# A gated mix of linear attention and a GEGLU feed-forward: order, halves and queues of the first loads, and q beside k

## The chip, the core and the metric

The kernel runs on one core of a Trainium2 chip. The core has TensorE (PE in the profile, with its weight loads as PEld), VectorE (DVE), ScalarE (ACT), GpSimd (POOL) and SyncE (SP), which run side by side and wait for each other by semaphores. SP and ACT issue the DMAs here. The metric is the device time of one launch in microseconds (us), the median over several launches.

## The reference

```python
def _A_ref(x, wqkv, wo):
    qkv = (x @ wqkv).reshape(B, S, 3, H, Dh).transpose(2, 0, 3, 1, 4)
    q, k, v = qkv[0], qkv[1], qkv[2]
    phi = lambda t: jnp.where(t > 0, t + 1, jnp.exp(t)) + 1e-6
    pq, pk = phi(q), phi(k)
    kv = jnp.einsum("bhsd,bhse->bhde", pk, v)
    z = jnp.einsum("bhsd->bhd", pk)
    num = jnp.einsum("bhqd,bhde->bhqe", pq, kv)
    den = jnp.einsum("bhqd,bhd->bhq", pq, z)[..., None] + 1e-6
    return (num / den).transpose(0, 2, 1, 3).reshape(B, S, D) @ wo

def _B_ref(x, w_gate, w_up, w_down):
    return (_gelu(x @ w_gate) * (x @ w_up)) @ w_down

x = A_x                      # S = 2048 rows, D = 640, H = 32 heads of 20, F = 1728
g = _sigmoid((x * gate_w).sum(-1, keepdims=True))
return g * _A_ref(x, A_wqkv, A_wo) + (1 - g) * _B_ref(x, B_w_gate, B_w_up, B_w_down)
```

All inputs and the output are bf16.

## The kernel before

The 2048 rows of x are 16 tiles of 128 rows; the 640 columns are 5 chunks of 128 (index k). Every matmul with x needs x transposed, with its columns on the partitions: this is xT. There are two ways into it. For the first NXN = 3 tiles, x is loaded as it is (L337) and T(i) (L396) transposes it with five TensorE transposes into a PSUM bank, from where a DVE copy (L406) takes it into xT. The other 13 tiles come by a transposing DMA each, issued by SP (load_xT, L340).

The work then goes in stages: phi(k) and phi(q) (L391 to L490); the products of phi(k) with x, from which kv and z are derived (MM and ME, from L495); the feed-forward's gate and up matmuls (G, L595), with the rest of the attention woven in (KV, W2, N); the output (FA, FB_half and FB). Only the first stage and its loads are touched by the change.

In the first stage, KM(i, ks) (L411) does, for tile i and each chunk k in ks, a pair of matmuls with the same weights, of 512 and 128 columns of wk; five pairs make a tile of k. QM(i) (L424) does the same with wq, whose chunk has one more column: the gate weights, put there by a small transpose and a DVE copy (L464 to L468). Each tile's result lies in a pair of PSUM banks (slot, L393): four pairs of banks in turn, though the first three tiles use the first three pairs and tile 3 the last. phi1(n) (L437) is ScalarE's Exp of it, with a Tanh of the gate column for a q tile; phi2(n) (L447) is two DVE instructions that make phi and store it, which frees the banks.

Everything is written down by hand in program order. P.op puts an instruction into its engine's list with the buffers it reads and writes; the planner works out the waits from these. Every engine runs its list in order, so an instruction that waits holds up all that is behind it on its engine. Waits are by whole buffers as named: the five chunks of wk are five names, wq is one, each tile of xT is one.

The order at the start: ACT issues the gate column, then the five chunks of wk (L334 to L336). SP issues x tiles 0 to 2 (L337, L338), then the 13 transposing DMAs (L345), then the rest of x in two pieces (L347 to L350), wg, wu, wv, wo. These later loads have no waits but SP's own order. On TensorE, warm (L382) first does a few matmuls with constants, whose results nobody reads, and then (L457 to L474):

```python
warm(6, 512); T(0); warm(2, 128); T(1); warm(2, 128)
KM(0, [0]); T(2)        # then the gate column's transpose
KM(1, [0])
for k in range(1, KC):
    KM(0, [k]); KM(1, [k]); KM(2, [k - 1])
KM(2, [KC - 1])
```

After that come k of tiles 3 to 15 and q of tiles 0 to 15, each with all five chunks (L475 to L481). wq is loaded as one transfer from ACT's queue, issued behind phi of tile 3 (L483). late_constants (L366), put down after tile 6, is work for POOL that waits for nothing but POOL.

Of the kernel before, what the change touches and what calls it, by code (L numbers as in the profile page):

```python
# [14 lines left out]
NT = S // 128  # L15
KC = D // 128
# [3 lines left out]
EPS = 1e-6  # L20
XW = 656

NXN = 3

class _Res:
    __slots__ = ("name", "writer", "readers", "excl", "lo", "hi", "idx", "fresh")
# [133 lines left out]
def bass_gated_mix__linear_attn_block__geglu_ffn__prompt_kernel(  # L160
# [24 lines left out]
    R_XT = take(KC * S)  # L185
# [36 lines left out]
    with (  # L222
# [8 lines left out]
        with contextlib.ExitStack() as stack:  # L231
# [65 lines left out]
            r_xone = P.sb("xone", R_XN, R_XN + NT * XW)  # L297
            r_pk = [P.sb("pk%d" % i, R_PK + i * 640, R_PK + (i + 1) * 640) for i in range(NT)]
            r_xT = [P.sb("xT%d" % i, R_XT, R_XT + KC * S) for i in range(NT)]
            r_wk = [P.sb("wk%d" % k, R_WK + k * 640, R_WK + (k + 1) * 640) for k in range(KC)]  # L300
            r_wq = P.sb("wq", R_WQ, R_WQ + KC * XW)
            r_gcol = P.sb("gcol", R_WQ, R_WQ + KC * XW)
            r_wv = P.sb("wv", R_WV, R_WV + KC * 640)
            r_wg = P.sb("wg", R_WG, R_WG + KC * 1664)
# [24 lines left out]
            def dma_in(dst, src, writes, reads=(), eng="sp"):  # L329
                P.op(eng, lambda e, dst=dst, src=src: e.dma_start(dst, src),  # L330
                     reads=reads, writes=writes, dma=new_dma_key())


            dma_in(gw_sb[0:5, :], gate_w.rearrange("(k p) -> k p", p=128), [r_gw], eng="act")  # L334
            for k in range(KC):
                dma_in(wk[:, k, :], A_wqkv[k * 128:(k + 1) * 128, 640:1280], [r_wk[k]], eng="act")  # L336
            for i in range(NXN):  # L337
                dma_in(x_aug[:, i, 0:640], A_x[0, i * 128:(i + 1) * 128, :], [r_xn[i]])  # L338

            def load_xT(i, after=()):  # L340
                P.op("sp", lambda e: e.dma_start_transpose(xT[:, :, i * 128:(i + 1) * 128],
                                                           A_x[0, i * 128:(i + 1) * 128, :]),
                     reads=list(after), writes=[r_xT[i]], dma=new_dma_key())

            for i in range(NXN, NT):  # L345
                load_xT(i)
# [44 lines left out]
            SLOTS = [(0, 1), (2, 3), (4, 5), (6, 7)]  # L391

            def slot(n):  # L393
                return SLOTS[n] if n < 3 else SLOTS[n % 4]

            def T(i):  # L396
                tb = 6 + i % 2

                def fn(e):
                    last = None  # L400
                    for k in range(KC):
                        last = e.transpose(psb[:, tb, k * 128:(k + 1) * 128],
                                           x_aug[:, i, k * 128:(k + 1) * 128], ident)
                    return last
                P.op("pe", fn, reads=[r_xn[i], r_ident], writes=[bank[tb]])
                P.op("dve", lambda e: e.tensor_copy(  # L406
                    xT[:, :, i * 128:(i + 1) * 128],
                    psb[:, tb, 0:640].rearrange("p (k s) -> p k s", k=KC)),
                    reads=[bank[tb]], writes=[r_xT[i]])

            def KM(i, ks):  # L411
                b0, b1 = slot(i)

                def fn(e):
                    last = None
                    for k in ks:
                        lhs = xT[:, k, i * 128:(i + 1) * 128]
                        e.matmul(ps[:, b0, :], lhs, wk[:, k, 0:512], start=(k == 0), stop=(k == KC - 1))  # L418
                        last = e.matmul(ps[:, b1, 0:128], lhs, wk[:, k, 512:640],  # L419
                                        start=(k == 0), stop=(k == KC - 1))  # L420
                    return last
                P.op("pe", fn, reads=[r_xT[i]] + [r_wk[k] for k in ks], writes=[bank[b0], bank[b1]])

            def QM(i):  # L424
                b0, b1 = slot(NT + i)

                def fn(e):
                    last = None
                    for k in range(KC):
                        lhs = xT[:, k, i * 128:(i + 1) * 128]  # L430
                        e.matmul(ps[:, b0, :], lhs, wq[:, k, 0:512], start=(k == 0), stop=(k == KC - 1))  # L431
                        last = e.matmul(ps[:, b1, 0:129], lhs, wq[:, k, 512:641],  # L432
                                        start=(k == 0), stop=(k == KC - 1))
                    return last
                P.op("pe", fn, reads=[r_xT[i], r_wq, r_gcol], writes=[bank[b0], bank[b1]])

            def phi1(n):  # L437
                b0, b1 = slot(n)
                m = n % 4
                P.op("act", lambda e: e.activation(e_buf[m], ps_flat[:, b0 * 512:b0 * 512 + 640], ACT.Exp),  # L440
                     reads=[bank[b0], bank[b1]], writes=[r_e[m]])
                if n >= NT:
                    i = n - NT
                    P.op("act", lambda e: e.activation(eg[:, i:i + 1], ps[:, b1, 128:129], ACT.Tanh, scale=0.5),
                         reads=[bank[b1]], writes=[r_eg[i]])

            def phi2(n):  # L447
                b0, b1 = slot(n)
                m = n % 4
                P.op("dve", lambda e: e.tensor_scalar(e_buf[m], e_buf[m], 1.0, EPS, ALU.min, ALU.add),  # L450
                     reads=[r_e[m]], writes=[r_e[m]])
                dst, r_dst = (pk[n], r_pk[n]) if n < NT else (pq[n - NT], r_pq[n - NT])
                P.op("dve", lambda e: e.scalar_tensor_tensor(  # L453
                    dst, ps_flat[:, b0 * 512:b0 * 512 + 640], 1.0 + EPS, e_buf[m], ALU.add, ALU.max),
                    reads=[bank[b0], bank[b1], r_e[m]], writes=[r_dst])

            warm(6, 512)  # L457
            T(0)
            warm(2, 128)
            T(1)  # L460
            warm(2, 128)
            KM(0, [0])
            T(2)
            P.op("pe", lambda e: e.transpose(psb[:, 7, 0:5], gw_sb[0:5, :], ident[0:5, 0:5]),  # L464
                 reads=[r_gw, r_ident], writes=[bank[7]])
            P.op("dve", lambda e: e.tensor_copy(wq[:, :, 640:641],
                                                psb[:, 7, 0:5].rearrange("p (k o) -> p k o", o=1)),
                 reads=[bank[7]], writes=[r_gcol])  # L468
            KM(1, [0])
            for k in range(1, KC):  # L470
                KM(0, [k])
                KM(1, [k])
                KM(2, [k - 1])
            KM(2, [KC - 1])  # L474
            for n in range(2 * NT):  # L475
                if n >= NT:
                    QM(n - NT)
                elif n >= 3:
                    KM(n, list(range(KC)))
                phi1(n)  # L480
                phi2(n)  # L481
                if n == 3:
                    dma_in(wq[:, :, 0:640], A_wqkv[:, 0:640].rearrange("(k p) w -> p k w", p=128), [r_wq],  # L483
                           eng="act")
                if n == 6:
                    late_constants()
            P.op("dve", lambda e: e.tensor_scalar(gg, eg, 0.5, 0.5, ALU.mult, ALU.add),
                 reads=r_eg, writes=[r_g])
# [316 lines left out]
```

## Time and profile before

| | us |
|---|---|
| median of 14 runs (276.66 to 278.55) | 277.27 |
| the profiled execution | 277.81 |
| span of the profiled execution | 276.5 |
| q and k tiles on TensorE, to the start of L502 | 51.37 |
| ACT issues of wk, five, first at | 1.40 |
| SP issues of the 13 transposing DMAs, first at 2.19, together | 21.09 |
| Exp of a tile (L440), mean of 32 | 0.703 |
| the two DVE instructions of a tile (L450, L453), means | 0.324 and 0.825 |
| DVE copy of a transposed tile (L406) | 0.49 |

The span is the time from the first to the last instruction that the profiler saw; what the launch adds lies around it. Times in the timeline are counted from the start of the span. A time in brackets behind an instruction is how long its engine was idle before it, with what released it. A DMA's time to landing counts from its issue until its semaphore says that all has arrived.

### The profile page before, as it was taken

The numbers are of one execution on the slowest core, as the hardware profiler recorded it, in microseconds if no ns is written. First come the engines' busy times: TensorE is split into PE (matmuls) and PEld (weight loads), VectorE is DVE, ScalarE is ACT, GpSimd is POOL, SyncE is SP. The second block draws the span as 40 slices with busy tenths as digits, with TensorE's granted clock in tenths as the row PEclk, the third lists the DMA queues.
The fourth block names the chain that finished last, engine by engine and source line by source line (L and its number), as shares of the span: only waits on it lengthen the run. The fifth ranks groups of instructions, "written<-read, shape, count | busy, mean of one in ns | idle before, by whom it ended". The sixth has DMA issues, their size and how long they took to land.

```text
span 276.5 us, 4070 instructions
## 1 busy us (share of the span) xinstructions
PE 271.9 (98%) x1696; PEld 140.2 (51%) x1696; DVE 138.5 (50%) x233; ACT 78.2 (28%) x132; POOL 26.1 (9%) x28
## 2 busy tenths in 40 slices
PE   7999999999999999999999999999999999999997
PEld 3455555555545444444444444444555555555553
DVE  1398888610243324999999999625100122212223
ACT  1354555310332354222232222323555100000000
POOL 5000000000000400332423322000000000000000
DMA  7998998002030212121221212390000011111111
GB/s 170 165 185 217 396 401 287 14 0 50 1 71 2 47 50 71 24 47 30 43 48 24 47 34 40 55 314 14 0 0 2 3 47 47 47 50 47 50 39 56
DMA packets 36401, 22.38 MB, mean 81 GB/s; under 512 B 25760, under 2 KB 34976, under 8 KB 36384
## 3 DMA queue, kind: packets, MB, share of 16 engines
q1 hardware_dynamic: 34997, 20.49, 27.9%
q10 hardware_dynamic: 1386, 1.64, 2.5%
q8 instruction: 13, 0.21, 0.4%
q14 instruction: 5, 0.03, 0.0%
HBM read 13.11 MB, written 2.62 MB: 57 GB/s over the span
## 4 chain that ended last, share of the span: by engine, by line
PE 95%; DMA 3%; ACTq 1%; DVE 0%; issue 0%
PE ps L595 41%; PE ps L738 20%; PE ps L701 6%; PE ps L431 6%; PE ps L502 6%; PE ps L418 6%; DMA pool<-in_A_wqkv_dram 3%; PE ps L504 2%; PE ps L432 2%; PE ps L702 2%; PE ps L570 2%; PE ps L419 1%; PE ps L722 1%; ACTq L330 1%; PE ps L616 1%; PE ps L632 1%
## 5 line engine op out<-in xcount | busy, mean ns | idle before, releaser
L595 PE MATMUL ps<-pool 128*128 128x512 bf16 x520 | 113.7, 379 | 0.0
L595 PEld LDWEIGHTS ps<-pool 128*128 128x128 bf16 x520 | 50.4, 98 | 60.0 <-issue 0.3
L738 PE MATMUL ps<-pool 128*128 128x512 bf16 (+1 forms) x416 | 57.2, 299 | 0.0
L603 DVE TENSOR_TENSOR pool<-ps,pool 128x512 bf16<-128x512 f32 x52 | 35.7, 687 | 33.6 <-PE ps L595 30.4
L601 ACT ACTIVATE pool<-ps 128x512 f32<-128x512 f32 x52 | 31.0, 597 | 72.5 <-PE ps L595 72.5
L749 DVE SCALAR_TENSOR_TENSOR pool<-ps,pool 128x512 bf16<-128x512 f32 (+1 forms) x32 | 16.2, 547 | 63.8 <-PE ps L738 63.8
L738 PEld LDWEIGHTS ps<-pool 128*128 128x128 bf16 x416 | 31.9, 98 | 25.2 <-issue 1.1
L647 POOL TENSOR_TENSOR pool<-pool 128x640 f32<-128x640 bf16 x16 | 22.5, 1408 | 141.0 <-DMA pool<-z_row 87.8
L440 ACT ACTIVATE pool<-ps 128x640 bf16<-128x640 f32 x32 | 22.3, 703 | 24.0 <-PE ps L419 14.4
L453 DVE SCALAR_TENSOR_TENSOR pool<-ps,pool 128x640 bf16<-128x640 f32 x32 | 26.4, 825 | 2.2
L655 DVE TENSOR_TENSOR pool<-pool 128x640 bf16<-128x640 bf16 x16 | 23.1, 1442 | 0.6
L418 PE MATMUL ps<-pool 128*128 128x512 bf16 x80 | 22.5, 383 | 0.6 <-DMA pool<-in_A_wqkv_dram 0.5
L431 PE MATMUL ps<-pool 128*128 128x512 bf16 x80 | 21.9, 379 | 0.0
L502 PE MATMUL ps<-pool 128*128 128x512 bf16 x80 | 21.9, 379 | 0.0
L701 PE MATMUL ps<-pool 128*128 128x512 bf16 x80 | 21.8, 379 | 0.0
L419 PE MATMUL ps<-pool 128*128 128x128 bf16 x80 | 17.6, 220 | 0.0
L432 PE MATMUL ps<-pool 128*128 128x129 bf16 x80 | 17.6, 220 | 0.0
L504 PE MATMUL ps<-pool 128*128 128x129 bf16 x80 | 17.6, 220 | 0.0
L702 PE MATMUL ps<-pool 128*128 128x128 bf16 x80 | 17.5, 219 | 0.0
L706 ACT ACTIVATE pool<-ps,pool 128x640 f32<-128x640 f32 x16 | 12.7, 793 | 9.2 <-PE ps L702 9.2
L450 DVE TENSOR_SCALAR pool<-pool 128x640 bf16<-128x640 bf16 x32 | 10.4, 324 | 7.4 <-ACT pool L440 5.7
L418 PEld LDWEIGHTS ps<-pool 128*128 128x128 bf16 x80 | 7.9, 98 | 10.3 <-DMA pool<-in_A_wqkv_dram 0.8
(51 smaller groups left out, 130.2 us busy)
## 6 DMA issues: line engine op xcount, KB each, us to landing
out_dram<-pool SPq DMA_DIRECT2D x15, 160.0 KB, 1.8
pool<-in_B_w_gate_dram SPq DMA_DIRECT2D x1, 2080.0 KB, 13.7
pool<-in_B_w_up_dram SPq DMA_DIRECT2D x1, 2080.0 KB, 18.4
pool<-in_A_x_dram SPq DMA_DIRECT2D x1, 1280.0 KB, 8.4
pool<-in_B_w_down_dram SPq DMA_DIRECT2D x1, 1120.0 KB, 5.7
pool<-in_A_wo_dram SPq DMA_DIRECT2D x6, 160.0 KB, 8.8
pool<-in_B_w_down_dram SPq DMA_DIRECT2D x1, 960.0 KB, 8.1
pool<-in_A_wqkv_dram ACTq DMA_DIRECT2D x5, 160.0 KB, 5.0
```

The costliest lines, as they stand in the source:

```text
L418: e.matmul(ps[:, b0, :], lhs, wk[:, k, 0:512], start=(k == 0), stop=(k == KC - 1))
L431: e.matmul(ps[:, b0, :], lhs, wq[:, k, 0:512], start=(k == 0), stop=(k == KC - 1))
L432: last = e.matmul(ps[:, b1, 0:129], lhs, wq[:, k, 512:641], start=(k == 0), stop=(k == KC - 1))
L453: P.op("dve", lambda e: e.scalar_tensor_tensor(dst, ps_flat[:, b0 * 512:b0 * 512 + 640], 1.0 + EPS, e_buf[m], ALU.add, ALU.max), reads=[ba ...
L502: e.matmul(ps[:, bs[n], :], lhs, x_aug[:, i, 0:512], start=(i == 0), stop=(i == NT - 1))
L504: last = e.matmul(ps[:, bt, n * 129:(n + 1) * 129], lhs, x_aug[:, i, 512:641], start=(i == 0 and n == 0), stop=(i == NT - 1), skip_group_c ...
L595: last = e.matmul(ps[:, b, :], w[:, k, fc * 128:(fc + 1) * 128], xT[:, k, j * 512:(j + 1) * 512], start=(k == 0), stop=(k == KC - 1))
L601: P.op("act", lambda e: e.activation(ge[n], ps[:, gb, :], ACT.Gelu_apprx_tanh), reads=[bank[gb]], writes=[r_ge[n]])
L603: P.op("dve", lambda e: e.tensor_tensor(hT[fc][:, j * 512:(j + 1) * 512], ps[:, ub, :], ge[n], ALU.mult), reads=[bank[ub], r_ge[n]], write ...
L655: P.op("dve", lambda e: e.tensor_tensor(pq[i].rearrange("p (h d) -> p h d", h=32), pq[i].rearrange("p (h d) -> p h d", h=32), den[n].unsqu ...
L701: e.matmul(ps[:, b0, :], lhs, w2[:, m, 0:512], start=(m == 0), stop=(m == KC - 1))
L738: last = e.matmul(dst, lhs, wd[:, fc, c0:c0 + cn], start=False, stop=(fc == NFC - 2), skip_group_check=True)
```

## The change

NXN becomes 2, so tile 2 comes by a transposing DMA and there are 14 of these. The early loads (x tiles 0 and 1, the chunks of wk, and wq in two pieces of two and three chunks) are each split into partitions 0 to 63, issued by SP, and 64 to 127, issued by ACT (halves). Their order on both queues is x0, wk0, x1, wk1 to wk4, on ACT the gate column, then wq. wq is thus issued ahead of the transposing DMAs, no longer behind phi of tile 3. Each half has a name of its own to wait for, and wq has one for each chunk.

T takes a list of chunks and a bank: tile 0 is transposed in two pieces, the first chunk alone. A list, seq, gives the order of tiles: k0, k1, q0, q1, and from tile 2 on k and q of a tile in turn; slot goes by the position in it. The order of the first pairs is written anew, the gate column's transpose (gate_col) moves behind the fourth chunk of k1, and QM takes a list of chunks. There are five heating matmuls instead of six and one group of two small ones instead of two.

```diff
--- before.py
+++ after.py
@@ -20,7 +20,8 @@
 EPS = 1e-6
 XW = 656
 
-NXN = 3
+NXN = 2
@@ -297,8 +298,12 @@
             r_xone = P.sb("xone", R_XN, R_XN + NT * XW)
             r_pk = [P.sb("pk%d" % i, R_PK + i * 640, R_PK + (i + 1) * 640) for i in range(NT)]
             r_xT = [P.sb("xT%d" % i, R_XT, R_XT + KC * S) for i in range(NT)]
+            r_xn_hi = [P.res("xnh%d" % i) for i in range(NXN)]
+            r_wk_hi = [P.res("wkh%d" % k) for k in range(KC)]
+            r_wq_hi = [P.res("wqh%d" % k) for k in range(KC)]
+            r_x0a = P.sb("x0a", R_XT, R_XT + 128)
             r_wk = [P.sb("wk%d" % k, R_WK + k * 640, R_WK + (k + 1) * 640) for k in range(KC)]
-            r_wq = P.sb("wq", R_WQ, R_WQ + KC * XW)
+            r_wq = [P.sb("wq%d" % k, R_WQ + k * XW, R_WQ + k * XW + 640) for k in range(KC)]
             r_gcol = P.sb("gcol", R_WQ, R_WQ + KC * XW)
...
@@ -331,16 +336,42 @@
                      reads=reads, writes=writes, dma=new_dma_key())
 
 
+
+            def load_x(i, eng):
+                dma_in(x_aug[:, i, 0:640], A_x[0, i * 128:(i + 1) * 128, :], [r_xn[i]], eng=eng)
+
+            def load_wk(k, eng):
+                dma_in(wk[:, k, :], A_wqkv[k * 128:(k + 1) * 128, 640:1280], [r_wk[k]], eng=eng)
+            def halves(dst, src, r_lo, r_hi):
+                dma_in(dst[0:64], src[0:64], r_lo)
+                dma_in(dst[64:128], src[64:128], r_hi, eng="act")
+
+            def load_x(i):
+                halves(x_aug[:, i, 0:640], A_x[0, i * 128:(i + 1) * 128, :], [r_xn[i]], [r_xn_hi[i]])
+
+            def load_wk(k):
+                halves(wk[:, k, :], A_wqkv[k * 128:(k + 1) * 128, 640:1280], [r_wk[k]], [r_wk_hi[k]])
+
+            def load_wq(k0, k1):
+                halves(wq[:, k0:k1, 0:640],
+                       A_wqkv[k0 * 128:k1 * 128, 0:640].rearrange("(k p) w -> p k w", p=128),
+                       r_wq[k0:k1], r_wq_hi[k0:k1])
+
+            load_x(0)
+            load_wk(0)
+            load_x(1)
+            for k in range(1, KC):
+                load_wk(k)
             dma_in(gw_sb[0:5, :], gate_w.rearrange("(k p) -> k p", p=128), [r_gw], eng="act")
-            for k in range(KC):
-                dma_in(wk[:, k, :], A_wqkv[k * 128:(k + 1) * 128, 640:1280], [r_wk[k]], eng="act")
-            for i in range(NXN):
-                dma_in(x_aug[:, i, 0:640], A_x[0, i * 128:(i + 1) * 128, :], [r_xn[i]])
-
-            def load_xT(i, after=()):
+            load_wq(0, 2)
+            load_wq(2, KC)
+
+            def load_xT(i):
                 P.op("sp", lambda e: e.dma_start_transpose(xT[:, :, i * 128:(i + 1) * 128],
                                                            A_x[0, i * 128:(i + 1) * 128, :]),
-                     reads=list(after), writes=[r_xT[i]], dma=new_dma_key())
+                     writes=[r_xT[i]], dma=new_dma_key())
 
             for i in range(NXN, NT):
                 load_xT(i)
@@ -391,25 +422,29 @@
             SLOTS = [(0, 1), (2, 3), (4, 5), (6, 7)]
 
             def slot(n):
-                return SLOTS[n] if n < 3 else SLOTS[n % 4]
-
-            def T(i):
-                tb = 6 + i % 2
-
+                return SLOTS[n % 4]
+
+            def T(i, ks, tb):
                 def fn(e):
                     last = None
-                    for k in range(KC):
-                        last = e.transpose(psb[:, tb, k * 128:(k + 1) * 128],
+                    for n, k in enumerate(ks):
+                        last = e.transpose(psb[:, tb, n * 128:(n + 1) * 128],
                                            x_aug[:, i, k * 128:(k + 1) * 128], ident)
                     return last
-                P.op("pe", fn, reads=[r_xn[i], r_ident], writes=[bank[tb]])
+                P.op("pe", fn, reads=[r_xn[i], r_xn_hi[i], r_ident], writes=[bank[tb]])
                 P.op("dve", lambda e: e.tensor_copy(
-                    xT[:, :, i * 128:(i + 1) * 128],
-                    psb[:, tb, 0:640].rearrange("p (k s) -> p k s", k=KC)),
-                    reads=[bank[tb]], writes=[r_xT[i]])
-
-            def KM(i, ks):
-                b0, b1 = slot(i)
+                    xT[:, ks[0]:ks[-1] + 1, i * 128:(i + 1) * 128],
+                    psb[:, tb, 0:len(ks) * 128].rearrange("p (k s) -> p k s", k=len(ks))),
+                    reads=[bank[tb]], writes=[r_x0a if i == 0 and ks[0] == 0 else r_xT[i]])
+
+
+            seq = [("k", 0), ("k", 1), ("q", 0), ("q", 1)]
+            for i in range(2, NT):
+                seq += [("k", i), ("q", i)]
+
+            def KM(n, ks):
+                i = seq[n][1]
+                b0, b1 = slot(n)
 
                 def fn(e):
                     last = None
@@ -419,28 +454,31 @@
                         last = e.matmul(ps[:, b1, 0:128], lhs, wk[:, k, 512:640],
                                         start=(k == 0), stop=(k == KC - 1))
                     return last
-                P.op("pe", fn, reads=[r_xT[i]] + [r_wk[k] for k in ks], writes=[bank[b0], bank[b1]])
-
-            def QM(i):
-                b0, b1 = slot(NT + i)
+                P.op("pe", fn, reads=[r_x0a if i == 0 and ks == [0] else r_xT[i]] + [r_wk[k] for k in ks] + [r_wk_hi[k] for k in ks],
+                     writes=[bank[b0], bank[b1]])
+
+            def QM(n, ks):
+                i = seq[n][1]
+                b0, b1 = slot(n)
 
                 def fn(e):
                     last = None
-                    for k in range(KC):
+                    for k in ks:
                         lhs = xT[:, k, i * 128:(i + 1) * 128]
                         e.matmul(ps[:, b0, :], lhs, wq[:, k, 0:512], start=(k == 0), stop=(k == KC - 1))
                         last = e.matmul(ps[:, b1, 0:129], lhs, wq[:, k, 512:641],
                                         start=(k == 0), stop=(k == KC - 1))
                     return last
-                P.op("pe", fn, reads=[r_xT[i], r_wq, r_gcol], writes=[bank[b0], bank[b1]])
+                P.op("pe", fn, reads=[r_xT[i], r_gcol] + [r_wq[k] for k in ks] + [r_wq_hi[k] for k in ks],
+                     writes=[bank[b0], bank[b1]])
 
             def phi1(n):
                 b0, b1 = slot(n)
                 m = n % 4
                 P.op("act", lambda e: e.activation(e_buf[m], ps_flat[:, b0 * 512:b0 * 512 + 640], ACT.Exp),
                      reads=[bank[b0], bank[b1]], writes=[r_e[m]])
-                if n >= NT:
-                    i = n - NT
+                kind, i = seq[n]
+                if kind == "q":
                     P.op("act", lambda e: e.activation(eg[:, i:i + 1], ps[:, b1, 128:129], ACT.Tanh, scale=0.5),
                          reads=[bank[b1]], writes=[r_eg[i]])
 
@@ -449,40 +487,49 @@
                 m = n % 4
                 P.op("dve", lambda e: e.tensor_scalar(e_buf[m], e_buf[m], 1.0, EPS, ALU.min, ALU.add),
                      reads=[r_e[m]], writes=[r_e[m]])
-                dst, r_dst = (pk[n], r_pk[n]) if n < NT else (pq[n - NT], r_pq[n - NT])
+                kind, i = seq[n]
+                dst, r_dst = (pk[i], r_pk[i]) if kind == "k" else (pq[i], r_pq[i])
                 P.op("dve", lambda e: e.scalar_tensor_tensor(
                     dst, ps_flat[:, b0 * 512:b0 * 512 + 640], 1.0 + EPS, e_buf[m], ALU.add, ALU.max),
                     reads=[bank[b0], bank[b1], r_e[m]], writes=[r_dst])
 
-            warm(6, 512)
-            T(0)
-            warm(2, 128)
-            T(1)
+            def gate_col():
+                P.op("pe", lambda e: e.transpose(psb[:, 7, 0:5], gw_sb[0:5, :], ident[0:5, 0:5]),
+                     reads=[r_gw, r_ident], writes=[bank[7]])
+                P.op("dve", lambda e: e.tensor_copy(wq[:, :, 640:641],
+                                                    psb[:, 7, 0:5].rearrange("p (k o) -> p k o", o=1)),
+                     reads=[bank[7]], writes=[r_gcol])
+
+
+            ALLK = list(range(KC))
+            warm(5, 512)
+            T(0, [0], 7)
+            T(0, [1, 2, 3, 4], 6)
             warm(2, 128)
             KM(0, [0])
-            T(2)
-            P.op("pe", lambda e: e.transpose(psb[:, 7, 0:5], gw_sb[0:5, :], ident[0:5, 0:5]),
-                 reads=[r_gw, r_ident], writes=[bank[7]])
-            P.op("dve", lambda e: e.tensor_copy(wq[:, :, 640:641],
-                                                psb[:, 7, 0:5].rearrange("p (k o) -> p k o", o=1)),
-                 reads=[bank[7]], writes=[r_gcol])
+            T(1, ALLK, 7)
+            KM(0, [1])
+            KM(0, [2])
             KM(1, [0])
-            for k in range(1, KC):
-                KM(0, [k])
-                KM(1, [k])
-                KM(2, [k - 1])
-            KM(2, [KC - 1])
+            KM(1, [1])
+            KM(1, [2])
+            KM(0, [3])
+            KM(1, [3])
+            gate_col()
+            KM(0, [4])
+            KM(1, [4])
             for n in range(2 * NT):
-                if n >= NT:
-                    QM(n - NT)
-                elif n >= 3:
-                    KM(n, list(range(KC)))
+                if n == 2:
+                    for k in range(3):
+                        QM(2, [k])
+                        QM(3, [k])
+                    QM(2, [3, 4])
+                    QM(3, [3, 4])
+                elif n > 3:
+                    (KM if seq[n][0] == "k" else QM)(n, ALLK)
                 phi1(n)
                 phi2(n)
-                if n == 3:
-                    dma_in(wq[:, :, 0:640], A_wqkv[:, 0:640].rearrange("(k p) w -> p k w", p=128), [r_wq],
-                           eng="act")
-                if n == 6:
+                if n == 8:
                     late_constants()
             P.op("dve", lambda e: e.tensor_scalar(gg, eg, 0.5, 0.5, ALU.mult, ALU.add),
                  reads=r_eg, writes=[r_g])
```

The first load_x and load_wk in the diff are replaced by the ones below them and are not called.

## The prediction

> **What bounds the kernel now.** I read the page's head and its chain that ended last, then the start of the timeline, then transfers and stretches of half a microsecond.
>
> ```profile
> span 276.5 us, 4070 instructions
> PE 271.9 (98%) x1696; PEld 140.2 (51%) x1696; DVE 138.5 (50%) x233; ACT 78.2 (28%) x132; POOL 26.1 (9%) x28
> PE 95%; DMA 3%; ACTq 1%; DVE 0%; issue 0%
> ```
>
> TensorE is the bound for the whole span. Its work is untouched by the diff except at the start, so a saving can only be time in which it does not do wanted matmuls. The chain says where that is: 3% of it is one transfer. In the timeline:
>
> ```profile
> 0.80 1.35 SPq L330 DMA_DIRECT2D pool<-in_A_x_dram  x3
> 0.83 2.72 PE L386 MATMUL ps<-const-bfloat16-1.0 128*128 128x512 bf16 x6 [0.83 <-PEq L790]
> 1.40 2.30 ACTq L330 DMA_DIRECT2D pool<-in_A_wqkv_dram  x5
> 2.19 21.09 SPq L341 DMA_TRANSPOSE pool<-in_A_x_dram  x13
> 4.84 0.63 PE L418 MATMUL ps<-pool 128*128 128x512 bf16 x1
> 6.68 0.45 PE L402 MATMUL ps<-pool 128*128 128x128 bf16 x5 [1.10 <-DMA pool<-in_A_x_dram]
> 9.72 0.39 PE L418 MATMUL ps<-pool 128*128 128x512 bf16 x1 [0.48 <-DMA pool<-in_A_wqkv_dram]
> 13.00 0.39 PE L418 MATMUL ps<-pool 128*128 128x512 bf16 x1
> 13.20 0.39 ACTq L330 DMA_DIRECT2D pool<-in_A_wqkv_dram  x1
> ...
> 21.40 0.10 PEld L418 LDWEIGHTS ps<-pool 128*128 128x128 bf16 x1 [0.41 <-DVE pool L450]
> 51.37 0.38 PE L502 MATMUL ps<-pool 128*128 128x512 bf16 x1
> ```
>
> A pair of matmuls (512 and 128 columns) starts every 0.272 us. The q and k projections are 160 pairs, 43.5 us, and the next stage starts at 51.37: 7.9 us of this stage are no pairs. Up to 4.84 TensorE heats itself and transposes; it does one pair, waits for x tile 2 until 6.68 and for the fourth wk chunk until 9.72. The twentieth pair is over at 13.00. Near 21.2 (a pair due at 21.16 starts at 21.43) it loses 0.27; the release is put down to DVE, but that tile is the eighth transposing DMA's, which lands then. Why the data is late:
>
> ```profile
> 4.50:5.00 0.50, 0.50 (x7) 0.49 (x5) 0.25 (x2) 0.50 (x1) 0.03 (x1) 1.00 0.90 316
> 5.50:6.00 0.50, 0.08 (x1) 0.00 (x0) 0.00 (x0) 0.00 (x0) 0.00 (x0) 1.00 1.07 123
> 20.00:20.50 0.50, 0.50 (x5) 0.31 (x4) 0.50 (x1) 0.50 (x1) 0.00 (x0) 1.00 0.06 6
> ```
>
> and of single issues (size, then us from issue to landing):
>
> ```profile
> pool<-in_A_wqkv_dram ACTq DMA_DIRECT2D x1, 160.0 KB, 6.9
> pool<-in_A_x_dram SPq DMA_TRANSPOSE x1, 8.0
> ```
>
> The last number of a stretch is GB/s; summed from 1.5 on, 0.89 MB have moved by 5.0. Plain loads run at some 330; from 5.0 on, when the transposing DMAs of x have reached the DMA engines, the sum is 94 to 230. The fourth wk chunk, issued at 2.75, takes 6.9 us, the first transposing DMA 8.0. Alone, transposing DMAs land 0.6 us apart (10.2 to 12.0). When wq (800 KB, issued at 13.20, 6.2 us) is done at 19.4, next to nothing moves for 1.5 us, and the eighth one lands at 21.2.
>
> **What the Trainium skill says.** "DMA: Bandwidth & Descriptors", section "Queues, rings and completion order": SP and ACT have each one ring on each of the same 16 DMA engines; a ring is worked in order, and an engine goes round its rings by packets. The trace agrees: half of those 0.89 MB is SP's three x tiles, and just then transposes, next in SP's ring, start to slow ACT's wk. The same page, "Rules for kernel authors", says of two transfers to disjoint partition halves "Don't bother"; no run here shows it. I give the split no bandwidth: it changes who issues what. "TensorE: Matmul & The Clock Gate", Part 1, says that the array runs at half rate until some 4 us of activity, the moment varying by about 0.5 us. The trace agrees: five transposes take 0.74 at 4.09 and 0.45 at 6.68.
>
> **The change part by part.**
>
> *Issue.* SP now issues nine plain loads before its first transposing DMA, seven of 80 KB, then wq in two. At 0.43 to 0.45 us each (1.35 for three) the first transposing DMA moves from 2.19 to about 4.8. ACT issues the other halves and the gate column: ten by 0.46, over at some 5.5. The table load behind them (1.28, at 3.73 before) ends at 6.8; the first Exp is due at some 8. Free. The tail of SP's queue moves later: fourteen transposing DMAs at 1.32 and about 1.5 us of stalls end near 25 instead of 23.3. x rows are wanted at 49 and were landing 5.6 to 8.4 us after issue; wg and wu are wanted at 70 and were landed by 48. Free, with over 10 us of cover.
>
> *Data.* In front of the transposes lie 1.97 MB: x 0.33, wk 0.82, wq 0.82. With 0.89 by 5.0 and 330 GB/s after (391 was seen in 16.5 to 17.0), the last byte is there at 7.8 to 8.3, plus some 0.5 to 1 us until it counts as landed. So wk comes every 0.5 us from about 4.2 on, all by some 6.6, against 10.2; the last wq piece lands at 8.8 to 9.3.
>
> *TensorE's start.* Five heating matmuls instead of six: over at 2.98, x0 still at 3.1, no gain. The first transpose is copied alone: 0.31 for it from 3.16, then the DVE copy. The trace has none of 128 columns; it lies between 0.17 (5 columns) and 0.49 (640), I take 0.23. It hides behind the other four transposes and two heaters. First pair at some 4.2, set by wk0, not 4.84. Then at half rate: this pair 0.53, the transposes of x1 0.53, the second pair 0.53, the third 0.40 across the clock's change: 6.2. Five pairs at 0.272: 7.56; the gate column's transpose (moved behind k=3 of tile 1, its load now behind ACT's seven halves, here by about 6.6) 0.1; two pairs: 8.2. The ten q pairs, 2.72: 10.9. Four of these use the first wq piece, so the second is due at 9.3, and tile 2's transposing DMA at 10.9.
>
> *The new waits.* Tile 2 comes by transposing DMA now. Bounds: alone, the last one took 2.9 us from issue; with first data at 8, that is 9.5. At worst the first one's 8.0 repeats: 4.8 + 8.0 = 12.8. A q pair waiting for wq, or k of tile 2 waiting for x, holds up everything on TensorE. I take 0.35 us of stall for both together, since ACT's ring (0.4 us behind by the gate load) keeps some 50 to 80 KB beside the first transposes: twentieth pair at 11.3.
>
> *The alternation.* k and q in turn consume a transposed tile every 2.72 us instead of 1.36; SP issues one each 1.32. So no later stall, and the 0.27 at 21.2 goes, as wq no longer runs among the transposes. ACT has 0.70 + 0.70 + 0.17 and DVE 4 instructions, 2.3 us, per 2.72: both as before on average, with four bank pairs in turn. Pool's constants do not wait for anything that moved: free.
>
> *Sum.* 13.00 − 11.3 + 0.27 = 2.0 us off this stage, and all behind it slides with TensorE. The profiled execution took 277.81 (1.3 outside the span), the median of the runs is 277.27; I subtract from the median: 275.3.
>
> **Rivals.**
>
> *Everything in time.* wq and tile 2 are there when wanted and the clock changes at 5.6: twentieth pair at 10.5, gain 2.8, 274.5. For it: transposes alone move 160 KB in 0.6 us. Against: two dates met with nothing to spare.
>
> *The first transposing DMA is late.* It lands at 12.8 as worked out above. Gain 13.00 − 12.85 + 0.27 = 0.4: 276.9. For it: the first one before took 8.0, and landed only when the last plain load did. Against: it had 0.42 MB of plain loads beside it, now less than 0.1.
>
> *wq crawls beside the transposes, slower.* Mechanism: SP's ring comes to the transposes while ACT's still holds its last wq half. ACT's wk moved some 0.36 MB in 5 us then, 72 GB/s. If 0.25 MB are left at 7.6, wq lands at 11.1; if also ACT's earlier half is left (0.4 MB), at 13.2; six q pairs (1.63) end at 14.8, with k of tile 2 after them: 1.5 later than 13.27, 278.8. It decides from a wq landing later than 11.6. For it: both occasions in the trace on which plain loads met transposes. Against: the rings get equal shares and SP's wq is in front of its own transposes.
>
> *The halves do nothing:* then the order alone carries the gain; this is in the forecast already.
>
> **How the numbers follow.** 0.2% of 277.27 is 0.55 us, about what a measurement of this kernel can tell from no change. Forecast 275.3 (its own range 274.4 to 276.4): 0.62. All in time: 0.14. First transpose late: 0.10, which is no measurable change. wq crawling: 0.14. So faster 0.76, same 0.10, slower 0.14. The range, 274.1 to 277.2, leaves out the outer half of the good case and most of the slow one.
>
> **What would show it.** Right: wk landings no longer spread to 10.2, no wait on x or wk over 0.3 us, the next stage starting near 49.4, no gap at 21. Wrong: a wait of TensorE of over 1 us on wq or on tile 2 between 8 and 13; half rate beyond 7; a wait for x rows or wg in later stages.

## The result and the profile after

The changed kernel takes 280.46 us (median of 10 runs, 280.03 to 281.54), the kernel before 277.29 (48 runs, 276.16 to 278.69): a ratio of 1.0114, 95% interval 1.0099 to 1.0129. It is 3.2 us slower, where 2.0 us less were forecast, and outside the range. The profiled execution took 281.11, its span is 279.8, 3.3 more than before.

From the page of the changed kernel, its head and its chain by engine:

```profile
span 279.8 us, 4070 instructions
PE 272.4 (97%) x1688; PEld 139.7 (50%) x1688; DVE 138.5 (49%) x233; ACT 78.2 (28%) x132; POOL 26.1 (9%) x28
PE 94%; DMA 3%; ACTq 2%; DVE 0%; issue 0%
```

TensorE is still the bound, and the chain still goes through one DMA of wqkv at the start. ACTq, time in which ACT only issues loads, is 2% of the chain instead of 1%. From the timeline of the changed kernel (start, duration; in brackets the idle time before and what ended it):

```profile
2.67 3.87 SPq L335 DMA_DIRECT2D pool<-in_A_wqkv_dram  x6
2.94 2.56 ACTq L335 DMA_DIRECT2D pool<-in_A_wqkv_dram  x4
5.54 0.86 ACTq L335 DMA_DIRECT2D pool<-in_gate_w_dram  x1
6.43 1.32 ACTq L335 DMA_DIRECT2D pool<-in_A_wqkv_dram  x2
6.58 20.65 SPq L372 DMA_TRANSPOSE pool<-in_A_x_dram  x14
7.89 0.62 PE L453 MATMUL ps<-pool 128*128 128x512 bf16 x1
8.40 0.38 PE L453 MATMUL ps<-pool 128*128 128x512 bf16 x1
11.98 0.38 PE L468 MATMUL ps<-pool 128*128 128x512 bf16 x1 [1.84 <-DMA pool<-in_A_wqkv_dram]
14.27 0.38 PE L468 MATMUL ps<-pool 128*128 128x512 bf16 x1 [1.04 <-DMA pool<-in_A_wqkv_dram]
15.90 0.38 PE L453 MATMUL ps<-pool 128*128 128x512 bf16 x1
54.00 0.38 PE L549 MATMUL ps<-pool 128*128 128x512 bf16 x1
```

SP issues its six loads of wk and wq 0.64 us apart, ACT its four likewise, where five whole chunks of wk came 0.46 apart before. SP comes to its first transposing DMA at 6.58, ACT to the two halves of wq at 6.43. TensorE waits for these halves twice, 2.9 us in all; the twentieth pair ends at 15.90 instead of 13.00. From there 140 pairs run without a gap (38.10 us, 0.272 each) to the next stage at 54.00, 2.63 later than before.

A stretch of time (the last two numbers are the busy share of the DMA engines and GB/s) and a single issue (last half of wq, issued at 7.12), both of the changed kernel:

```profile
2.50:9.50 7.00, 6.02 (x32) 2.83 (x31) 1.14 (x3) 1.28 (x1) 1.83 (x4) 1.00 0.87 229
```

```profile
pool<-in_A_wqkv_dram ACTq DMA_DIRECT2D x1, 240.0 KB, 7.0
```

The plain loads come at 229 GB/s, not at 330, while the DMA engines are counted busy for 0.87 of the time. From 2.5 to 6.5, before the first transposing DMA is issued, it is 227 already. The last half lands at 14.1.

The remaining 0.67 us lie at the other end. From the last 4 us of the changed kernel, and below it of the kernel before, transfers and last store:

```profile
q14 instruction: 1, 0.01, 0.8%
...
out_dram<-pool SPq DMA_DIRECT2D x1, 32.0 KB, 2.3
```

```profile
out_dram<-pool SPq DMA_DIRECT2D x1, 32.0 KB, 1.6
```

From the end of the last DVE instruction to the end of the span are 2.35 us (277.45 to 279.8), before 1.67 (274.83 to 276.5). A transfer of instructions runs beside the last store, and the store lands 0.7 later.

### The profile page after: what moved, and what is told of

Its sections match the earlier page's. It is cut to its first block, busy times and chain, and to the rows that moved or that the text cites. A ratio compares the mean times of both kernels' runs of the same rounds, so it can differ in the third digit from the quotient of the medians.

```text
span 279.8 us, 4070 instructions
## 1 busy us (share of the span) xinstructions
PE 272.4 (97%) x1688; PEld 139.7 (50%) x1688; DVE 138.5 (49%) x233; ACT 78.2 (28%) x132; POOL 26.1 (9%) x28
## 4 chain that ended last, share of the span: by engine, by line
PE 94%; DMA 3%; ACTq 2%; DVE 0%; issue 0%
PE ps L642 40%; PE ps L785 20%; PE ps L748 6%; PE ps L549 6%; PE ps L468 6%; PE ps L453 5%; DMA pool<-in_A_wqkv_dram 3%; ACTq L335 2%; PE ps L551 2%; PE ps L749 2%; PE ps L469 2%; PE ps L617 2%; PE ps L454 1%; PE ps L769 1%; PE ps L663 1%; PE ps L679 1%
## 5 line engine op out<-in xcount | busy, mean ns | idle before, releaser
L642 PE MATMUL ps<-pool 128*128 128x512 bf16 x520 | 113.7, 379 | 0.0
L468 PE MATMUL ps<-pool 128*128 128x512 bf16 x80 | 23.5, 379 | 2.9 <-DMA pool<-in_A_wqkv_dram 2.9
L453 PE MATMUL ps<-pool 128*128 128x512 bf16 x80 | 24.7, 394 | 0.6 <-DMA pool<-in_A_wqkv_dram 0.6
L549 PE MATMUL ps<-pool 128*128 128x512 bf16 x80 | 21.9, 379 | 0.0
L748 PE MATMUL ps<-pool 128*128 128x512 bf16 x80 | 21.8, 379 | 0.0
L488 DVE TENSOR_SCALAR pool<-pool 128x640 bf16<-128x640 bf16 x32 | 10.4, 326 | 7.8 <-ACT pool L478 6.6
```

Of the source, the lines that this page charges most:

```text
L549: e.matmul(ps[:, bs[n], :], lhs, x_aug[:, i, 0:512], start=(i == 0), stop=(i == NT - 1))
L642: last = e.matmul(ps[:, b, :], w[:, k, fc * 128:(fc + 1) * 128], xT[:, k, j * 512:(j + 1) * 512], start=(k == 0), stop=(k == KC - 1))
L748: e.matmul(ps[:, b0, :], lhs, w2[:, m, 0:512], start=(m == 0), stop=(m == KC - 1))
```

## The experiments

All times are medians. A ratio is a version's time over that of the kernel before on the same chip (277.0 to 277.4), with its 95% interval in brackets. Dates and rates come from one profiled execution of each version.

**Each early load whole, the two queues in turn**

```diff
-                dma_in(dst[0:64], src[0:64], r_lo)
-                dma_in(dst[64:128], src[64:128], r_hi, eng="act")
+                dma_in(dst, src, list(r_lo) + list(r_hi), eng=("sp", "act")[turn[0] % 2])
+                turn[0] += 1
```

> The changed kernel with each early load whole (128 partitions) and the two queues in turn: x0, x1, wk2, wk4 and wq's chunks 2 to 4 on SP, wk0, wk1, wk3, the gate column and wq's chunks 0 and 1 on ACT. Theory A (the halves cost issue time: 0.64 us each on both queues, so 160 KB come per 0.64 us, and ACT's wq is issued so late that it meets the transposing DMAs): issue is over by 3.5 us, the first transposing DMA issued near 3.5 instead of 6.6, wq landed by 9.5, twentieth pair at 11.3 to 12, time 275.3 to 276.2. Rival B (wq beside transposing DMAs crawls however it is issued): wq's piece on ACT lands after 11.5, TensorE waits for it over 1.5 us, time 278.5 to 281.

Measured: 277.12, ratio 1.0000 (0.9985 to 1.0014). The 3.2 us are gone, the late last store (1.6 us here) among them. Its timeline and its rate:

```profile
1.71 1.38 SPq L335 DMA_DIRECT2D pool<-in_A_wqkv_dram  x3
3.14 1.32 SPq L374 DMA_TRANSPOSE pool<-in_A_x_dram  x1
8.28 0.63 PE L455 MATMUL ps<-pool 128*128 128x512 bf16 x1
8.81 0.39 PE L455 MATMUL ps<-pool 128*128 128x512 bf16 x1
```

```profile
2.50:7.50 5.00, 4.31 (x23) 2.44 (x22) 1.14 (x3) 1.28 (x1) 1.83 (x4) 1.00 1.05 371
```

Issue (0.46 each) and landing (wq at 8.6 and 9.0) are as theory A had them, with no wait on wq. The time is not: TensorE runs at half rate until 8.7, and the twentieth pair ends at 12.58. So in this execution the forecast's dates for the data hold, while its date for the clock was early. Three more versions with all loads whole follow under "TensorE's clock" (two with the gate column moved); in them the data came later.

**Only x and wk whole; only wq whole**

```diff
# x and wk whole (wk2 and wk4 on SP, the others of wk on ACT)
-                halves(x_aug[:, i, 0:640], A_x[0, i * 128:(i + 1) * 128, :], [r_xn[i]], [r_xn_hi[i]])
+                dma_in(x_aug[:, i, 0:640], A_x[0, i * 128:(i + 1) * 128, :], [r_xn[i], r_xn_hi[i]])
...
# wq whole, the rest in halves
-                halves(wq[:, k0:k1, 0:640],
+                dma_in(wq[:, k0:k1, 0:640],
...
-                       r_wq[k0:k1], r_wq_hi[k0:k1])
+                       r_wq[k0:k1] + r_wq_hi[k0:k1], eng="act" if k0 == 0 else "sp")
```

> The changed kernel with x and wk whole and only wq in halves. Theory A: x and wk are there as early as with all loads whole (wk by 6.3); wq's halves are issued by 4.5 us and move at 240 to 260 GB/s, ACT's last half partly beside the transposes: landed at 10 to 11, TensorE waits 0.5 to 1.5 us, time 277.5 to 278.7. Rival C (wq's halves alone are the cost): 280 to 281, as the changed kernel.

> The changed kernel with only wq's two pieces whole (chunks 0 and 1 on ACT, 2 to 4 on SP); x and wk stay in halves. Theory A (halves move slowly, some 240 GB/s against 370, and what counts is that wq's last half is left beside the transposing DMAs): wq's SP piece is in front of the transposes and lands by 10.5, the ACT piece (half the bytes that ACT had left) by 11.5; TensorE waits 1 to 1.5 us for it instead of 2.9; time 278.5 to 279.5. Rival C (the cost lies in wq's halves alone, those of x and wk are harmless): 277.0 to 277.8, as with all loads whole.

With x and wk whole: 276.70, ratio 0.9988 (0.9975 to 1.0001). wq's last half lands at 10.0 and costs one wait, as theory A had it; the time is lower than it had, and rival C is out:

```profile
10.10 0.38 PE L469 MATMUL ps<-pool 128*128 128x512 bf16 x1 [0.64 <-DMA pool<-in_A_wqkv_dram]
```

So the seven halves of x and wk on each queue are enough for the whole loss of the first stage: without them the next stage starts at 49.82, in the kernel before at 51.37. wq's halves move slowly too (213 to 264 GB/s from 6.0 to 8.5), but are issued by 4.3 instead of 7.8.

With only wq whole: 282.76, ratio 1.0195 (1.0159 to 1.0230), worse than either expectation. Two lines of its timeline show where:

```profile
11.69 0.18 PE L497 MATMUL ps<-pool 5*128 5x5 bf16 x1 [2.48 <-DMA pool<-in_gate_w_dram]
12.30 0.63 PE L453 MATMUL ps<-pool 128*128 128x512 bf16 x1
```

The gate column, 1.2 KB issued at 5.56, lands only at 11.6, TensorE waits 2.48 and is at half rate again until 18: the granted TensorE clock of the profile (1.00 is full) is 0.50 from 11.4 to 18.2, and its mean over the span 0.988. Half of these 6.8 us, 3.4, is an estimate of the most that this cost; the time is 3.3 above theory A's range. Why so small a load takes 6 us there stays open.

**Halves along the columns**

```diff
-                dma_in(dst[0:64], src[0:64], r_lo)
-                dma_in(dst[64:128], src[64:128], r_hi, eng="act")
+                dma_in(dst[..., 0:320], src[..., 0:320], r_lo)
+                dma_in(dst[..., 320:640], src[..., 320:640], r_hi, eng="act")
```

> The changed kernel with the halves cut along the columns: 128 partitions of 320 columns on each queue, as many DMAs of as many bytes as before, rows of 640 bytes. If it is the 64 partitions that make halves slow (issue at 0.62 us, 240 GB/s): issue at 0.45 us, 300 GB/s or more, wq landed by 10, time 277 to 278. Rival (twice as many DMAs of 80 KB are slow in themselves): rate under 260 GB/s and time 279.5 to 281.

Measured: 278.07, ratio 1.0031 (1.0016 to 1.0046). Issue is at 0.39 to 0.49 (the 0.45 expected). The rate, over the stretch used above for the whole loads:

```profile
2.50:7.50 5.00, 3.73 (x21) 2.02 (x20) 1.14 (x3) 1.28 (x1) 1.83 (x4) 1.00 0.99 268
```

From 4.5 to 8.5 it is 303; from 3.5 to 4.5 it was 160, why is open. Row halves had 228 from 2.5 to 7.5, and the four executions with all loads whole 371, 311, 299 and 263 (the first experiment and three below). So the rate is above that of row halves, but not told apart from that of whole loads.

From column halves to row halves (280.46) are 2.4 us, and only the shape of a piece differs: 64 partitions of 640 columns instead of 128 of 320. From whole loads (277.12) to column halves are 0.95; of these some 0.65 are the late last store, which this version has too (2.2 us). The 0.3 that are left for more DMAs with shorter rows are within the intervals. wq's last piece lands at 11.3 here, not by 10; still TensorE does not wait for it, as its pairs are at half rate until 9.7.

**The first transposing DMA waits until wq has landed**

```diff
             for i in range(NXN, NT):
-                load_xT(i)
+                load_xT(i, after=r_wq + r_wq_hi if i == NXN else ())
```

> The changed kernel, with the first transposing DMA waiting on SP until all of wq has landed. If plain loads crawl because transposing DMAs run beside them: wq lands at 9.5 to 10.5 instead of 14.1, TensorE waits under 0.5 us for it, then for tile 2, issued at about 10 and landed 2.9 later at 13; twentieth pair before 12.8, k of tile 2 at 13, time 277.3 to 278. Rival (the halves' issue alone makes it late, nothing is due to the company of the transposing DMAs): wq lands at 13 to 14 all the same, tile 2 at 17, time 281 to 282.

Measured: 280.17, ratio 1.0111 (1.0087 to 1.0135). Neither number came out:

```profile
11.22 0.38 PE L468 MATMUL ps<-pool 128*128 128x512 bf16 x1 [1.18 <-DMA pool<-in_A_wqkv_dram]
14.95 0.38 PE L453 MATMUL ps<-pool 128*128 128x512 bf16 x1 [0.85 <-DMA pool<-in_A_x_dram]
```

Without company wq's last half lands at 11.9. Of its 4.8 us of delay against the forecast (14.1 against 9.3), 2.2 are thus due to the transposing DMAs beside it and 2.6 are there without them. Nor is slow issue all of these 2.6. Issue is over at 7.8 here and no transposing DMA is under way before 11.9, and yet:

```profile
8.00:10.00 2.00, 1.32 (x9) 0.51 (x7) 0.18 (x1) 1.28 (x2) 0.00 (x0) 1.00 1.03 244
```

Halves are both issued slowly and moved slowly; what each of the two costs was not separated. The wait moves what was won to tile 2, whose transposing DMA is issued at 11.9 and lands 2.9 later. The next stage starts at 53.04 instead of 54.00, but the median is only 0.3 lower than the changed kernel's, less than four runs can tell.

**The gate column's load last on ACT**

```diff
-            dma_in(gw_sb[0:5, :], gate_w.rearrange("(k p) -> k p", p=128), [r_gw], eng="act")
             load_wq(0, 2)
             load_wq(2, KC)
+            dma_in(gw_sb[0:5, :], gate_w.rearrange("(k p) -> k p", p=128), [r_gw], eng="act")
...
-            gate_col()
             KM(0, [4])
             KM(1, [4])
+            gate_col()
```

> The changed kernel with the gate column's load behind wq on ACT's queue, and its transpose behind the last pair of k1. Theory A': the gate load's 0.9 us of issue between wk4 and wq is what sets ACT's wq behind SP's; without it both wq pieces are issued 0.9 us earlier and land 1 to 2.5 us earlier (the last at 11.6 to 13.1 instead of 14.1), time 278 to 279.5. Rival B (the transposing DMAs alone decide): the last wq half lands within 0.5 us of 14.1, time 280.0 to 280.8.

Measured: 281.51, ratio 1.0169 (1.0129 to 1.0209). In the profiled execution the gate column lands at 12.1, TensorE waits 2.98 us for it, and no pair waits for wq after that; the next stage starts at 53.46 instead of 54.00. The last half of wq lands at 11.8 instead of 14.1, as theory A' had it, and the wait passes to the gate column. The median is no better. The trace is of the fastest of four runs: two took 280.55 and 280.72 at a mean granted clock of 1.000, two 282.30 and 282.53 at 0.994. So this shows only that moving that load wins nothing.

**The kernel before, with the first transposing DMA held until wk has landed**

```diff
             for i in range(NXN, NT):
-                load_xT(i)
+                load_xT(i, after=r_wk if i == NXN else ())
```

> The kernel before with one wait more: its first transposing DMA is issued only when all of wk has landed. If the transposing DMAs are what made x tile 2 and wk late there: wk all landed by 7 instead of 10.2, no wait for the fourth chunk, fifteenth pair at 9.3 instead of 11.6, tile 3 (issued near 7, landed near 10) costs a wait of 0.5 us, time 275.3 to 276. Rival (the plain loads were at their own pace and the transposes cost nothing): wk still lands near 10, the transposing DMAs come 8 us later and tile 3 near 13, time 278.5 to 280.

Measured: 280.70, ratio 1.0126 (1.0080 to 1.0172). wk is all landed at 6.8 instead of 10.2, as expected, the fifteenth pair ends at 10.4 instead of 11.6, and tile 3 costs no wait. But the transposing DMAs are now 4.8 us later, and wq, still issued behind tile 3's phi, runs into the fifth of them (issued at 12.26, landed at 18.6):

```profile
18.69 0.38 PE L418 MATMUL ps<-pool 128*128 128x512 bf16 x1 [2.68 <-DMA pool<-in_A_x_dram]
```

In the kernel before the same collision costs 0.27, since tiles had been landed ahead. So transposing DMAs do slow plain loads (wk at 10.2 with them, at 6.8 without), and a transposing DMA beside wq takes 6.3 us where one alone took 2.9; a wait that separates them in one place uses up the lead that hid them in the next. The trace, again of the fastest of the four runs (279.12, mean granted clock 1.000), accounts for 1.35 us, the later start of the next stage (52.72). The other three took 280.32 to 282.12 at 0.994; a stretch at half rate behind the wait, as with only wq whole, would fit this, but no trace shows it.

**TensorE's clock**

Three edits: the gate column first on ACT in the whole-load version (x0 lands at 3.2, not 3.8); seven heating matmuls instead of five, in the whole-load version and in that with x and wk whole; seven small ones instead of two behind T(0), with the gate column first.

```diff
-            warm(5, 512)
+            warm(7, 512)
```

> All early loads whole as in the first run, and the gate column's load first on ACT's queue. x0 then has the DMA engines to itself for half a microsecond and lands at 3.1 to 3.3 instead of 3.8, TensorE has no gap in front of the first transposes, and the first pair starts near 4.2. Theory D (the whole-load version is held by its late start and by TensorE at half rate until 8.7): the start comes 0.5 earlier and the clock's change, with a TensorE that is never idle, before 7.7; twentieth pair at 11.0 to 11.8, time 275.3 to 276.5. Rival (the loads' total sets the date, wq at 9): 276.9 to 277.3.

> All early loads whole as in the first run, and seven heating matmuls of 512 columns instead of five, so that TensorE has no gap between 3.1 and 3.8, where it waited for x0. Theory E (the clock changes only after a stretch[...] without a gap[...]; a gap of 0.6 us puts it off to 8.7): change by 7.7 at the latest, twentieth pair at 10.9 to 12, time 275.3 to 276.4, and less spread. Rival (the moment of the change does not depend on such gaps): 276.8 to 277.4, as without the two.

> x and wk whole, wq in halves, and seven heating matmuls instead of five. Theory E: 275.6 to 276.4. Rival: 276.5 to 276.9, as without the two.

> All early loads whole, the gate column first on ACT's queue, and seven small heating matmuls instead of two between the transposes of x0 and the first pair, where TensorE waited 0.58 for wk0. Theory E: the clock changes by 7.7 instead of 8.9, time 275.8 to 276.8. Rival: 277.5 to 277.9.

Measured, in this order: 277.73 (1.0022, 1.0007 to 1.0037); 276.78 (0.9979, 0.9966 to 0.9991); 276.27 (0.9966, 0.9954 to 0.9978); 277.65 (1.0019, 1.0006 to 1.0032). Only the third time is what its theory had; the fourth is what the rival had, the first lies above both ranges, the second between them. The gate column first, with x0 earlier, did not help: half rate lasted until 8.9 there, and with the gap filled the second wk chunk landed at 7.5 and TensorE waited for it. Without the gap before x0 the medians are 0.3 and 0.4 us lower than without the two matmuls (277.12 and 276.70), but the intervals overlap. In the profiles of these two full rate is there at 5.2 and 4.55; the latter's line:

```profile
4.55 0.38 PE L454 MATMUL ps<-pool 128*128 128x512 bf16 x1
```

In all four executions with seven heating matmuls (two more follow below) it was there by 5.9. But it was there at 4.6 to 5.1 in four versions with a gap as well, the one with x and wk whole among them, and at 8.3 to 9.7 in four others. That the gap decides is therefore not shown; the moment varies by some 5 us among executions with nearly the same start.

Nor does an early clock alone bring the forecast's time. With all loads whole and seven heating matmuls TensorE waits for data instead:

```profile
6.34 0.39 PE L455 MATMUL ps<-pool 128*128 128x512 bf16 x1 [0.70 <-DMA pool<-in_A_wqkv_dram]
9.71 0.38 PE L470 MATMUL ps<-pool 128*128 128x512 bf16 x1 [0.82 <-DMA pool<-in_A_wqkv_dram]
```

Its twentieth pair ends at 12.44, with five heating matmuls at 12.58. The loads are the same and issued at the same moments, but moved at 311 GB/s instead of 371 from 2.5 to 7.5, and wq's pieces landed at 9.6 and 9.8 instead of 8.6 and 9.0. In the two versions with the gate column first the rates were 299 and 263, and wq's last piece landed at 9.6 and 10.5. So the rate of the same loads varies from one execution to the next; why is open.

**The late last store**

Two edits of the fastest version (x and wk whole, seven heating matmuls): three chunks of wo loaded in two parts each by SP; four small loads more on ACT.

```diff
+                    for j in range(1, 5):
+                        r_ex.append(P.res("extra%d" % j))
+                        dma_in(gw_sb[8 * j:8 * j + 5, :], gate_w.rearrange("(k p) -> k p", p=128),
+                               [r_ex[-1]], eng="act")
```

> The kernel of the run before last (x and wk whole, wq in halves, seven heating matmuls) with three more DMA instructions on SP in the middle: three of wo's chunks, not due for 60 us, are loaded in two column halves each. SP then has as many instructions as in the changed kernel. Theory F (in the changed kernel SP fetches a last block of instructions, 0.01 MB on the instruction queue, beside its last store, and this is 0.65 us of its loss): the instruction transfer appears in the last 4 us, the last 32 KB store lands 2.2 to 2.3 after issue instead of 1.6, span and time 0.6 to 0.7 longer than without the three, 276.8 to 277.1. Rival (the late store of the changed kernel comes from something else): store 1.6, time 276.0 to 276.5.

> The kernel with x and wk whole, wq in halves and seven heating matmuls, with four more DMA instructions on ACT (the gate column once more, 1.2 KB each, to places that nothing reads, issued behind the ninth tile's phi, where ACT is idle half of the time; one DVE instruction at the end of the stage waits for them). ACT then issues ten loads, as in the changed kernel. Theory G (what is fetched beside the last store in the changed kernel hangs on the length of ACT's list, not SP's): an instruction transfer of 0.01 MB in the last 4 us, the last store at 2.2 to 2.3 us, time 276.8 to 277.1. Rival (not ACT's list either): no such transfer, the store 1.6, time 276.1 to 276.5.

With three more on SP: 276.33 (0.9966, 0.9954 to 0.9977), last store 1.6, no transfer of instructions beside it: theory F is out. With four more on ACT: 276.82 (0.9990, 0.9974 to 1.0007), as theory G had it, and in its last 3.6 us:

```profile
q14 instruction: 1, 0.01, 1.0%
...
out_dram<-pool SPq DMA_DIRECT2D x1, 32.0 KB, 2.3
```

The next stage starts 0.17 earlier than without the four (49.69 against 49.86), and the span is 0.6 longer. So it is the ten loads on ACT that bring this transfer about, not the length of SP's list. All five versions with ten on ACT have the transfer and a last store of 2.2 or 2.3; all others, with nine or fewer, have neither. That the transfer is what holds up the store is likely, not shown.

## Why the prediction was wrong

- *What bounds the kernel, and where it loses:* right. Only the first stage could give time, and each pair costs 0.272 throughout.
- *The step that failed* is the split into halves: "I give the split no bandwidth: it changes who issues what". The split was put at nothing, and it cost the whole loss, 3.2 us. The Trainium skill's "Don't bother" ("DMA: Bandwidth & Descriptors", "Rules for kernel authors") speaks of nothing won; the runs show a loss. A load of 64 partitions mostly takes 0.60 to 0.62 us to issue, more than a whole one (0.37 to 0.46), so 160 KB come per 0.64 us with both queues at work. The loads also move slowly once issued (244 GB/s with the hold): from 2.5 to 7.5 at 228 GB/s, whole ones at 263 to 371.
- *Issue* ("0.43 to 0.45 us each") was nine times 0.64 on SP: the first transposing DMA at 6.58, not 4.8. ACT ended at 7.8, not 5.5.
- *Data:* "330 GB/s after" does not hold for halves (wq at 14.1 against 9.3). Of four executions with whole loads one is above it (371, wq landed at 9.0) and three are below (wq at 9.6 to 10.5), so the date was an early one for whole loads too.
- *TensorE's start:* the first pair at 4.59, not 4.2; half rate until 8.3, not 6.2. Neither costs anything in the changed kernel, where TensorE then waits for wq, but with whole loads the late clock is one reason why the twentieth pair ended at 12.58 and not at 11.3. It is not the only one: with the clock early, it ended at 12.44, since the data were late. The 0.5 us by which the prediction lets the clock's moment vary is far less than what these executions show (4.6 to 9.7).
- *The new waits:* 2.9 us, not 0.35. Tile 2 was feared for equally; its transposing DMA took 7.7 us, close to the 8.0 named as the worst, landed at 14.3 and was not waited for.
- *The alternation:* right, no later stall, and the 0.27 near 21 is gone.
- *The tail of the queues, "Free":* right for x and wg, but 0.67 us were added at the last store by three more loads on ACT (ten, before seven), which no row of the profile before could have priced.
- *The rivals:* "wq crawls beside the transposes, slower" is what happened: ACT's last half was the one left over, at 14.1, after the 11.6 named there. It had 0.14, and named ACT's lag without its cause. Its 278.8 lacked 1.1 us of wq's delay (k of tile 2 at 15.90, not 14.8) and the 0.67 at the store. "The halves do nothing" was taken as a floor, and so no rival priced them as a loss.
- *The sum* read 2.0 us off an execution of 277.81 and subtracted them from a median of 277.27. Here this matters: with x and wk whole the profiled execution took 1.6 us less than that of the kernel before (276.23), but the median only 0.5 less (276.70 against 277.23).

The fastest version tried, with x and wk whole on two queues, wq in halves, and seven heating matmuls, takes 276.27, ratio 0.9966 (0.9954 to 0.9978): 0.3% faster than the kernel before. The forecast's 275.3 was reached by none.

## What to carry to other kernels

Do not cut a load of 128 partitions into two of 64 to share it between two queues, which cost 3.2 us here: give the queues whole loads in turn. When two queues carry one operand, the later half decides; add up the issues of each queue with a duration for that shape, and take a shape the trace does not show as a possible loss too. Subtract a gain from the execution in whose trace it was read. A wait that keeps transposing and plain DMAs apart is worth only as much as the lead it leaves.

## What was not expected of the hardware

- Issuing 64 partitions of 640 columns took 0.55 to 0.62 us (ACT's second load 0.84), 128 of 640 or of 320 columns 0.37 to 0.46. Why is open. Without transposes beside them the row halves moved at 237 GB/s (2.5 to 9.5, with the hold). From 2.5 to 7.5 whole loads moved at 263 to 371 in four executions, column halves at 268 in one.
- TensorE came to full rate between some 4.6 and 9.7 us in executions with nearly the same start. In one, it fell back to half rate during a wait of 2.5 us and stayed there for 6.8 us; behind waits of 2.7 and 3.0 us in two others it was at full rate.
- Four DMA instructions more on ACT, issued in the first stage, brought a transfer of instructions beside the last store and 0.8 us more between the last DVE instruction and the end of the span.
